# Attention, transforms and the first FFN tiles issued along one written list instead of tables per step

## The chip, the core and the metric

The kernel runs on one core of a Trainium2 chip, as one program. The metric is device time in microseconds, from the launch to the end of the core. In the profile PE is TensorE's matmul side and PEld its weight loads, DVE is VectorE, ACT is ScalarE, POOL is GpSimd and SP is SyncE, which issues most of the DMAs.

## What is computed

Attention with a window of 128 and 4 sink tokens, for 4 batches of 8 heads over 768 tokens, then a Fourier mixing of the result, then a feed-forward network (FFN) with a residual. All in fp32.

```python
keep = is_sink | ((rel >= 0) & (rel < window))          # rel = i - j, sinks are j < 4
a = softmax(where(keep, scale * q @ k.T, -1e9)); x = a @ v   # 4 x 8 heads, S = 768, D = 64
X = fft(fft(x, axis=1), axis=2)                          # over tokens, then over the 512 channels
u = x + real(X)
un = (u - mean(u)) / sqrt(var(u) + 1e-6)
out = u + relu(un @ w_ch1) @ w_ch2                       # 512 -> 2048 -> 512
```

## The kernel before

**Attention.** A query block is 128 tokens; there are 24 (g = 0 to 23, six to a batch). Each block has four steps, one per pair of heads, so that step s stands for block s // 4 and pair s % 4, and 96 steps (and 14 more to drain) make the stage. At even steps `scores` makes the scores of two pairs in a PSUM tile `s` (two buffers). `merge` (VectorE, `copy_predicated`) picks between window and sink columns, `soft1` (VectorE) adds the mask and takes the row's minimum, `expo` (ScalarE) takes the exponential, `sink_p` (GpSimd) splits off the four sink columns. For every second pair `trans_p` turns four heads' weights on TensorE into PSUM tile `pt` (one buffer), `copy_p` (ScalarE) moves them to SBUF as `pta`, `newer_p` and `older_p` (GpSimd) cut them to the two key blocks, and `av` multiplies with V into `xt`. Per block `trans_sink` turns the sink weights, from block 8 on into the same tile `pt`, `copy_sink` moves them, `copy_x` moves `xt`, `turn_x` turns it back and adds the sinks' part, and `store_x` (VectorE) scales it into the token block `u`. A pair of blocks below is written g.pair: `trans_p` 8.3 is that of pairs 2 and 3 of block 8.

**Fourier transform.** When four of a batch's six blocks are stored, `fourier` enters the batch's work in a table `ev` under (step, engine): folds of the token blocks (`fold_n`, `fold_m` on VectorE and GpSimd, `fold_hi` on ScalarE, `fold_lo` on VectorE), stage 1 (`stage1`: products za, za, zr, zb, zb, each in up to two parts), the splits of its results (`z_hi` on ScalarE, `z_lo` on VectorE), stage 2 (`stage2a`, `stage2b`), and `combine` and `update`, which add the result to `u`. Products go to PSUM bank `fft`, or to bank `x` of the attention at certain steps.

**FFN.** 24 token blocks are worked in six groups of four. For an inner tile f (16 of them) `ch1` is 12 matmuls into PSUM tile `h`, `relu` (ScalarE) and `relu_lo` (VectorE) split the result in two, `ch2` is 12 matmuls into four accumulators `o`. `convert` brings a weight tile from 64-bit to 32-bit floats (three VectorE operations, L606 to L608), copies the high part (ScalarE) and subtracts the low one (GpSimd), and issues the next load. The first group runs while the last batches' transforms end. The other five groups run in a loop of their own from some 320 us on (from L1485 on).

**What sets the order.** Each engine works through its own queue in order. Up to step 96 the order is written out: the loop over s issues loads, then `scores`, then for each engine the row of `SCHEDULE[s >= 36]` for s % 4, an operation being called with its lag from `STEP_LAG` or `BLOCK_AT`, and the events of `ev` where the row says so. At `CUT` = 97 `man.close()` ends the written order; from there on the planner of the framework orders all that is issued, by its own costs, until the loop over the other groups, which is written out again. In the row for s % 4 = 3 TensorE has `trans_p`, the events, `av`, `trans_sink`, `turn_x`; `av` falls on even steps alone, so that only events can stand between `trans_p` and `trans_sink`.

## Time and profile before

| | us |
|---|---|
| median of three runs | 760.65 |
| the runs | 757.99, 760.65, 761.95 |
| the profiled execution | 760.99 |
| its span, first to last instruction | 759.3 |
| outside the span | 1.69 |

The profile is of one execution. A busy engine is not an engine at its peak: matmuls are pipelined and their ends are modelled. An idle time is put down to the instruction whose end released the waiting one. A granted clock of 1.00 is 2.4 GHz, one of 0.50 is 1.2 GHz; values between are the mean of a stretch that has both.

### The profile page before, as it was taken

Reading aid. Unit: us, or ns where it says so; the run is one execution under the profiler, and the core shown is the slowest. Engines: PE = TensorE matmul, PEld = TensorE weight load, DVE = VectorE, ACT = ScalarE, POOL = GpSimd, SP = SyncE. Lnnn points to the kernel's source line nnn. Section 1 sums busy time; section 2 is a strip of 40 time slices with the busy share of each in tenths; the row PEclk is TensorE's granted clock in tenths of the full one; section 3 lists DMA queues with packets and bytes.
Section 4 is the critical chain, followed back from the end, with each engine's and each line's share of the span. In section 5 each row is a group of like instructions: output and inputs, shape, how many; then the busy total and the mean of one; then the engine's idle time right before and its main releaser. Section 6 shows DMA issues by size and latency. Waiting matters only on the chain.

```text
span 759.3 us, 14752 instructions
## 1 busy us (share of the span) xinstructions
PE 727.4 (96%) x5223; PEld 626.7 (83%) x5223; DVE 598.6 (79%) x1630; ACT 345.2 (45%) x896; POOL 187.0 (25%) x289
## 2 busy tenths in 40 slices
PE   8987998989899999999999999999999999999995
PEld 6766876867688878788889898898999989898994
DVE  7997688889899789879787798677895798674435
ACT  5885776756543233345555334333443334333330
POOL 3675486577638254200000000000000000000001
PEclk9998999999999999999999999999999999999998
DMA  9982536433215266135447657656666566655761
GB/s 256 286 242 75 150 87 183 128 127 103 94 63 180 103 195 208 56 125 193 154 153 260 212 161 240 220 171 186 200 215 208 177 185 217 191 159 179 217 186 60
DMA packets 95306, 129.18 MB, mean 170 GB/s; under 512 B 5956, under 2 KB 60748, under 8 KB 94968
## 3 DMA queue, kind: packets, MB, share of 16 engines
q1 hardware_dynamic: 94216, 124.00, 51.8%
q0 software_dynamic: 720, 3.76, 1.5%
q8 instruction: 43, 0.70, 0.4%
q10 hardware_dynamic: 288, 0.39, 0.1%
q14 instruction: 39, 0.32, 0.1%
HBM read 104.00 MB, written 24.13 MB: 169 GB/s over the span
## 4 chain that ended last, share of the span: by engine, by line
PE 76%; DVE 16%; issue 2%; DMA 2%; ACT 2%; SPq 1%; POOL 1%; DVEq 0%; ACTq 0%; POOLq 0%
PE h L644 32%; PE p L1360 26%; PE xt L843 4%; PE o L1186 4%; PE s L738 3%; PE pt L805 2%; DVE sm L769 2%; DVE s L753 2%; PE za L402 2%; DVE f L369 1%; DVE gl L385 1%; PE zb L402 1%; DVE f L379 1%; PE a L429 1%; PE zr L402 1%
## 5 line engine op out<-in xcount | busy, mean ns | idle before, releaser
L1360 PE MATMUL p<-w_ring,h_sums 128*128 128x256 f32 x936 | 131.4, 282 | 0.0
L1360 PEld LDWEIGHTS p<-w_ring,h_sums 128*128 128x128 f32 x936 | 123.0, 188 | 3.5 <-DVE u L1190 0.2
L1308 ACT CAST h_sums<-sums 128x256 fp32r<-128x256 f32 (+2 forms) x158 | 89.8, 568 | 68.8 <-PE p L1360 30.6
L1309 DVE TENSOR_TENSOR h_sums<-sums,h_sums 128x256 fp32r<-128x256 f32 (+2 forms) x158 | 98.3, 622 | 17.7 <-ACT h_sums L1308 16.6
L1360 PE MATMUL p<-w2t,h_sums 128*128 128x256 f32 x702 | 110.3, 282 | 0.0
L1382 POOL TENSOR_TENSOR u<-u,u 128x512 f32<-128x512 f32 x3 | 3.8, 1288 | 425.3 <-DVE u L1382 425.3
L1360 PEld LDWEIGHTS p<-w2t,h_sums 128*128 128x128 f32 x702 | 97.6, 189 | 3.4
L644 PE MATMUL h<-un_slots,w 128*128 128x512 f32 x396 | 97.9, 395 | 0.0
L644 PE MATMUL h<-un_last,w 128*128 128x512 f32 x396 | 97.2, 394 | 0.0
L780 ACT ACTIVATE sm<-sm,mx 128x132 f32<-128x132 f32 x192 | 75.9, 399 | 23.0 <-DVE mx L769 22.4
L644 PEld LDWEIGHTS h<-un_slots,w 128*128 128x128 f32 x396 | 72.6, 188 | 15.1
L644 PEld LDWEIGHTS h<-un_last,w 128*128 128x128 f32 x396 | 72.2, 188 | 15.0 <-DVE un_slots L559 0.7
L1522 ACT ACTIVATE sums<-h 128x512 f32<-128x512 f32 x40 | 23.9, 598 | 98.8 <-PE h L644 98.8
L1210 DVE STREAM_TRANSPOSE unf<-un 32x128 f32<-32x128 f32 x192 | 58.0, 302 | 2.8
L1490 ACT ACTIVATE sums<-h 128x512 f32<-128x512 f32 x40 | 23.9, 599 | 67.6 <-PE h L644 67.6
L1319 DVE TENSOR_TENSOR sums<-sums 128x256 f32<-128x256 f32 x39 | 16.4, 421 | 48.4 <-ACT sums L1522 48.1
L769 DVE CUSTOM_DVE_ANT_0 sm<-s,mask 128x132 f32<-128x132 f32 x192 | 47.1, 289 | 3.2 <-DVE s L753 0.5
L843 PE MATMUL xt<-ptl,ldv 128*64 128x128 f32 x384 | 40.5, 297 | 1.0 <-issue 0.9
L738 PE MATMUL s<-ring,q 64*64 64x196 f32 (+1 forms) x640 | 37.7, 351 | 3.0 <-DVE mx L769 2.8
L753 DVE COPY_PREDICATED s<-other,s 64x256 f32<-64x256 uint8 x80 | 34.5, 431 | 5.6 <-PE s L738 2.9
L821 POOL TENSOR_SCALAR_AFFINE_SELECT ptl<-pta 128x512 f32<-128x512 f32 x48 | 32.2, 672 | 22.0 <-ACT pta L812 17.5
L780 ACT ACTIVATION_READ_ACCUMULATOR sm<-sm,mx 128x1 f32 x192 | 36.7, 191 | 0.0
(236 smaller groups left out, 1365.8 us busy)
## 6 DMA issues: line engine op xcount, KB each, us to landing
w_ring<-w2s SPq DMA_DIRECT2D x62, 512.0 KB
w2t<-w2s SPq DMA_DIRECT2D x93, 256.0 KB
raw<-in_moe_w_ch_dram SPq DMA_DIRECT2D x32, 512.0 KB
w2s<-w_ring SPq DMA_DIRECT2D x16, 512.0 KB
ldv<-in_v_dram SPq DMA_DIRECT2D x28, 256.0 KB
ring<-in_qk_dram SPq DMA_DIRECT2D x24, 264.0 KB
w2s<-w2t SPq DMA_DIRECT2D x24, 256.0 KB
out_dram<-u SPq DMA_DIRECT2D x22, 256.0 KB
```

Source lines behind the costliest of these rows:

```text
L402: T.matmul(ps[:, :NK], a, c, start=i == 0, stop=i == len(mm) - 1)
L644: T.matmul(ps[:, :tb], a[:, cs], x[:, :, cc, :], start=n == 0, stop=n == 3 * NCC - 1)
L738: T.matmul(ps[HC * x:HC * x + HC, j, c:c + k.shape[-1]], st["q", g][rows, hp + i, HC * x:HC * x + HC], k, start=True, stop=True)
L753: V.copy_predicated(part(rows, c_out), other[qi > 2][rows], part(rows, c_in))
L769: V.tensor_tensor_reduce(sm[:, h % 4], ps[:, j, c:c + W], mask[min(qi, 3)], -SCALE, 3.0e38, ALU.add, ALU.min, accum_out=mx[:, 0, h:h + 1])
L780: A.activation(sm[:, h % 4], sm[:, h % 4], AF.Exp, bias=mx[:, 0, h:h + 1], scale=-1.0, accum_out=mx[:, 1, h:h + 1])
L821: G.affine_select(lo, a, [[0, 4], [s, P]], compare_op=ALU.is_ge, fill=0.0, base=0, channel_multiplier=-s)
L843: T.matmul(ps[D * j:D * j + D, p, :], st["v", kb(g) - i][:, h, :], a[:, h % 4, :], start=i == 0, stop=i == n - 1)
L1210: V.transpose(unf[32 * q:32 * q + 32, :, r], un[r].rearrange("p (c q j) -> p c q j", c=NCC, q=4)[:, :, q])
L1308: A.copy(hc_hi[:, left(a, n)], src)
L1309: V.tensor_tensor(hc_lo[:, left(a, n)], src, f32(hc_hi[:, left(a, n)]), op=ALU.subtract)
L1360: T.matmul(acc[i][:, 2 * P * tp:2 * P * tp + 2 * P], x, w, start=q == 0 and tp == 0 and n == 0, stop=q == end and n == 2, skip_group_check ...
```

## The change

The loop over the steps no longer issues anything itself. A generator, `everything`, yields the same pieces of work in the order of the tables (each with its step, a name and a function), over all 110 steps and on through the first five inner tiles of the FFN's first group. The pieces are put in queues by a one-letter code (`CODES`), and then a string, `WORK`, of 1158 letters is read from left to right: each letter calls the next piece of its queue. So pieces of one code keep their order, and pieces of different codes stand as the string says. All of this lies within the written order; the planner comes in at the sixth inner tile (`F_LIST` = 5), no longer at step 97.

With it go some smaller edits. Events have more codes (`EVENTS`): the folds' casts are "B", the weight conversions "W", "E" and "I", where `convert` is cut in three (`join`, `join_hi`, `join_lo`), and so on. Which PSUM bank a transform's product takes is a letter too: T for `fft`, X for the attention's `x`, Y for the FFN's `n`; R is a `trans_sink` into `fft`. Tiles are made when their first piece runs (`part_of`, `Made`). The first two inner tiles put their `relu` into buffers of the attention (`pta`, `ptl`), since these are still open. The operations, their shapes and their engines are the same, and there are as many of them. Twelve of the letters T early in the list are pieces that issue nothing (`FILL` = 0), and the letters q near the end load nothing.

An example of how to read it: in the fourth row, `t f a V c G f e r m s` is `trans_p` 8.3, a `soft1`, `av` 8.1, a `fold_m`, `copy_p` 8.3, a `fold_n`, `soft1` 9.1, `expo` 9.0, `trans_sink` 8, `merge` 9.2, `scores` 10.0. By the tables TensorE has `trans_p` 8.3, `trans_sink` 8, `scores` 10.0, `av` 8.1 there, and ScalarE `expo` 9.0, `expo` 9.1, `copy_x` 7, `copy_p` 8.3; by the list ScalarE has `copy_x` 7, `copy_p` 8.3, `expo` 9.0.

```diff
-EVENTS = ("A", 0, 1, 2, 3, "V", "G", "T")
+EVENTS = {"A": "ABCE", 0: (0,), 1: (1,), 2: (), 3: (), "V": "VLOW", "G": "GHI", "T": "TNP"}
...
-ENGINES = ("S", "A", 0, 1, 2, 3, "V", "G", "T")
+ENGINES = ("S", "A", "B", "C", "E", 0, 1, "V", "L", "O", "W", "G", "H", "I", "T", "N", "P")
+F_LIST = 5
 EV_D, EV_Z = 0, 1
 X_AT, X_NOT = (2,), (81, 97)
+EVEN, ODD = ("merge",), ("sink_p", "trans_p", "copy_p", "newer_p", "older_p", "av")
+OLDER, FIRST = ("older_p", "merge"), ("sink_hi", "sink_lo")
+CODES = {
+    "load_qk": "q", "load_k": "k", "load_sink": "n", "load_v": "v", "S": "S", "scores": "s", "merge": "m", "soft1": "f", "expo": "e",
+    "sink_p": "i", "trans_p": "t", "copy_p": "c", "newer_p": "w", "older_p": "o", "av": "a", "copy_x": "x", "copy_sink": "y",
+    "trans_sink": "r", "turn_x": "u", "inverse": "d", "store_x": "z", "sink_hi": "h", "sink_lo": "l", "A": "A", "B": "B", "C": "C",
+    0: "D", 1: "Z", "W": "W", "E": "E", "I": "I", "P": "P", "banks": "0", "second": "1", "third": "3", "keep": "j", "relu": "J", "relu_lo": "K", "ch2": "2",
+    "V": "V", "L": "L", "O": "O", "G": "G", "H": "H", "T": "T", "N": "N", "M": "M",
+}
+OTHER = {"R": "r", "X": "T", "Y": "T"}
+WORK = (
+    "TsTTkqsTqTTvMTTTTTTTTTTTTTCMfeffsefVsveitmeqfcifetwmRscGfyaewftmeisvvcfaefwqVteoscmeitfwxRdyuocfeaiV"
+    "mwesqoftefiVsGzncRGmAeawfyteodvicfxVwsmqeuofhiVeafteVzRsmGciaywfeVdotvfxVmcseuwqfefoamivetzSiRfacdyf"
+    "weskltoxefsqvfuGcVieazAtwefVoRacdyeswftxVoemSuicsfviefawVqeGtzmRaciSyVswSxtfeduGfcamGesvvfBtwfeqVaos"
+    "cVeitxzcwamoRVuGyafedifBTwmeosqvVxitfaVcGfermsnyewztfoucdieafGmesqwvtfBofeViscTzewmxorfyuAidetfacmes"
+    "wqvZhtofiefTzcTmewrfsoAkdayieZXfxlefTfeidTAdeTZtiAucZswqvzTofeVGTfaVAetZiXcdGrsywAaBomtfxTfcewuAsSve"
+    "zTVGqmaDtifXHcfeVTwArsSyDeaVHmtxfTicfHeduAsvvewTzqomaitDGsVHcaBfferVTywxtemuocfsqeiVawfeztomsGnhcafe"
+    "fwmroxvsqyfHuefmetiaHcLesztGLacwfBtdovxfiVcsqweTmveoXLAiZTwforfTAmiyeTZeLaAiufedftezskaLciLwZrsLoqvy"
+    "lxTLfTeftLLXLcfAdwTfeZoaALietZLeLudLLcTizswLroVayGtmxTcufAfwesSvVTezGqmaiBGtVTcXAwfrsDSyeaHfeLtHmxTc"
+    "uLwTfsvvVAeoaVqTiftqqqqqqeDGszciTBHmNrVaCwTyxftedaoOcaGfAeVuwxTmsovDtiLHTfcVeraywfezsotmiGNfcadHCfBO"
+    "seVwuevmTxoLitAafcHerfzysemNwftoCdaciOewfueomsvxiZtLfTcfewzTemoNriafCdAaOyeZtf0edTWciTXAdETwZYoAWITt"
+    "ATcTZErZuAWTwyxTYAaDETzoWaIuxTVYAETITPDVAIVSSTJHPDVHzBKuJVVVVz1V2VBKVV2VVBVVTVV3jjYWAZAEHTZWIYAZEWTA"
+    "IPAZEZWITJYAKETWAPIDEVTJI2AKWHTPDEVIWTJ2AHKETWIDEVIWHEWIEI"
+)
...
+            other_bank = [None]
 
             def bank(b, name):
                 turn[0] += 1
-                if len(banks) == 1 and extra:
-                    t = extra[0](f"{name}_{b}")
-                    if t is not None:
-                        return t
+                if other_bank[0] == "X":
+                    return extra[0](f"{name}_{b}")
+                if other_bank[0]:
+                    pool, t, n = banks[other_bank[0] == "Y"]
+                    return pool.tile([P, 512], F32, tag=t, name=f"{name}_{b}", bufs=n)
                 pool, t, n = banks[turn[0] % len(banks)]
...
-                    at(k + F_S[0], "A", lambda j=j: fold_hi(j))
+                    at(k + F_S[0], "B", lambda j=j: fold_hi(j))
...
-                        pool, tag = (ps_fft, "fft") if NP * g + BLOCK_AT["trans_sink"] < PHASE else (ps_t, "pt")
+                        pool, tag = (ps_fft, "fft") if other_bank[0] == "R" else (ps_t, "pt")
...
-                    at(s + CONV_AT[i], "V", lambda i=i: convert(i))
+                    at(s + CONV_AT[i], "W", lambda i=i: join(i))
+                    at(s + CONV_AT[i] + 1, "E", lambda i=i: join_hi(i))
+                    at(s + CONV_AT[i] + 1, "I", lambda i=i: join_lo(i))
                 for f in range(2):
-                    at(s + CH1_AT[f], "T", lambda f=f: hp.append(ch1(0, f, unT0)))
-
-            hp = []
...
+                    h = [state["aw"].tile([P, tb], F32R, tag=t, name=f"{t}h_{f}", bufs=PTB) for t in ("pta", "ptl")]
...
-                        s = at_s = 0
-                        extra.append(lambda name: ps_t.tile([P, 512], F32, tag="x", name=name)
-                                     if at_s % NP in X_AT and not X_NOT[0] <= at_s <= X_NOT[1] and at_s < len(steps) - 2 else None)
-                        while s < last:
+                        def use(s, op, lag_):
+
+                            if 0 <= s - lag_ < len(steps):
+                                g, hp = steps[s - lag_]
+                                if op not in (EVEN if hp % 2 else ODD) and (g % NB or op not in OLDER):
+                                    yield op, lambda: table[op](g, hp)
+
+                        def use_block(s, op):
+
+                            g, k = divmod(s - BLOCK_AT[op], NP)
+                            if k == 0 and 0 <= g < NQ and (g % NB == 0 and g or op not in FIRST):
+                                yield op, lambda: table[op](g)
+                                if op == "store_x" and g % NB == 3:
+                                    b = g // NB
+                                    fourier(b, lambda d, e, f: at(s + d, e, f), FOLD_AT if b < B - 1 else FOLD_LAST)
+
...
+                        def work(s):
+
+                            yield from loads(s)
+                            yield from events(s, "S")
+                            if s < len(steps) and s % 2 == 0:
+                                yield "scores", lambda: scores(*steps[s])
                             if s == 0:
                                 a, b, e = SINK0_AT
-                                at(a, "A", lambda: sink_hi(0))
+                                at(a, "C", lambda: sink_hi(0))
                                 at(b, e, lambda: sink_lo(0))
                             for e in "AVGT":
-                                for op in SCHEDULE[s >= PHASE][e][k]:
+                                for op in SCHEDULE[s >= PHASE][e][s % NP]:
                                     if op in EVENTS:
-                                        run_ev(s, op)
+                                        for key in EVENTS[op]:
+                                            yield from events(s, key)
                                     elif op in STEP_LAG:
-                                        lag(table[op], s, STEP_LAG[op])
+                                        yield from use(s, op, STEP_LAG[op])
                                     else:
-                                        at_ = s - BLOCK_AT[op]
-                                        if at_ % NP == 0 and 0 <= at_ // NP < NQ:
-                                            table[op](at_ // NP)
-                                            if op == "store_x" and at_ // NP % NB == 3:
-                                                b = at_ // NP // NB
-                                                fourier(b, lambda d, e, f, s=s: at(s + d, e, f), FOLD_AT if b < B - 1 else FOLD_LAST)
-                            run_ev(s, "M")
-                            s += 1
+                                        yield from use_block(s, op)
+                            yield from events(s, "M")
...
+                            yield s, "second", second
+                            for f in range(F_LIST):
+                                if f > 1:
+                                    yield s, "P", lambda f=f: first_product(f)
+
+                                def relu_hi(f=f):
+                                    hs[f] = relu(0, f, hps[f])
+
+                                yield s, "relu", relu_hi
+                                yield s, "relu_lo", lambda f=f: relu_lo(0, hps.pop(f), hs[f])
+                                for _ in range(PER_F):
+                                    for e in ENGINES:
+                                        for op, fn in events(s, e):
+                                            yield s, op, fn
+                                    s += 1
+                                if f < 2 or f > 2:
+                                    j = f if f < 2 else f - 1
+                                    yield s, "ch2", lambda j=j: ch2(j, hs.pop(j), state["po"])
+                                if f == 1:
+                                    yield s, "third", third
+                                    for j in range(2):
+                                        yield s, "keep", lambda j=j: keep_w2(j)
+                                for i in () if f < 1 else range(4, 8) if f == 1 else range(2 * f + 4, 2 * f + 6):
+                                    yield s, "W", lambda i=i: join(i, state["wa"])
+                                    yield s, "E", lambda i=i: join_hi(i, state["wa"])
+                                    yield s, "I", lambda i=i: join_lo(i)
...
+                        for s, op, fn in everything():
+                            queues.setdefault(CODES[op], []).append(fn)
+                            plain.append(CODES[op])
+                            if op == "trans_sink" and s < PHASE:
+                                plain[-1] = "R"
+                            if op == "T" and s % NP in X_AT and not X_NOT[0] <= s <= X_NOT[1] and s < len(steps) - 2:
+                                plain[-1] = "X"
+                            if op == "T" and s > len(steps) + 2 and len(plain) % 2:
+                                plain[-1] = "Y"
+                        todo = {c: iter(q) for c, q in queues.items()}
+                        for c in WORK or plain:
+                            other_bank[0] = c
+                            next(todo[OTHER.get(c, c)])()
+                        other_bank[0] = None
+                        assert all(next(q, None) is None for q in todo.values())
```

## Rows read from the trace of the kernel before

**Rows 1.** The page: its line of busy times, and the granted clock in 40 slices
```profile
PE 727.4 (96%) x5223; PEld 626.7 (83%) x5223; DVE 598.6 (79%) x1630; ACT 345.2 (45%) x896; POOL 187.0 (25%) x289
...
PEclk9998999999999999999999999999999999999998
```

**Rows 2.** Busy time by stretch: PE, PEld, DVE, ACT, POOL, clock, DMA
```profile
0.00:205.00 205.00, 185.13 (x2001) 147.86 (x2001) 171.04 (x685) 141.97 (x527) 128.10 (x244) 0.96 0.53 160
205.00:250.00 45.00, 41.92 (x243) 36.53 (x244) 44.59 (x80) 15.84 (x32) 26.02 (x17) 1.00 0.33 111
...
320.00:759.30 439.30, 431.32 (x2663) 386.51 (x2661) 322.94 (x768) 165.35 (x300) 3.78 (x3) 0.99 0.58 185
```

**Rows 3.** What TensorE waited for until 330 us: total, times, longest
```profile
PE pk L862 <- ACT pta L812: 7.5, 6, 3.2
PE s L738 <- DVE mx L769: 2.8, 3, 1.2
PE a L429 <- DVE d L456: 2.1, 1, 2.1
...
PE a L429 <- DVE mx L769: 1.5, 1, 1.5
PE dc L429 <- DVE zb L417: 1.3, 1, 1.3
```

**Rows 4.** Stretches of 5 us with a low clock, columns as in rows 2
```profile
60.00:65.00 5.00, 1.60 (x17) 1.22 (x17) 4.76 (x21) 3.01 (x11) 3.19 (x9) 0.92 0.54 166
65.00:70.00 5.00, 5.00 (x39) 3.83 (x40) 2.37 (x11) 2.33 (x11) 1.88 (x4) 0.50 0.32 103
...
115.00:120.00 5.00, 2.79 (x37) 2.15 (x37) 4.79 (x24) 3.99 (x15) 4.77 (x11) 0.88 0.54 172
120.00:125.00 5.00, 5.00 (x45) 4.16 (x38) 3.41 (x10) 2.45 (x11) 1.99 (x3) 0.77 0.88 310
165.00:170.00 5.00, 4.95 (x44) 4.22 (x45) 4.21 (x14) 1.82 (x9) 3.98 (x6) 0.66 0.67 209
195.00:200.00 5.00, 3.48 (x25) 2.93 (x25) 4.95 (x17) 3.17 (x12) 3.51 (x4) 0.74 0.32 105
```

**Rows 5.** In order of time, the longest wait: start, us, engine, line, operation
```profile
62.98 0.08 DVE L769 DVE_READ_ACCUMULATOR2_ANT mx<- 128x1 f32 x1
...
64.14 0.58 ACT L812 COPY pta<-pt 128x512 f32<-128x512 f32 x1
...
64.86 0.34 PE L862 MATMUL pk<-ident_r,sk 128*128 128x128 f32 x1 [3.22 <-ACT pta L812]
...
65.13 1.61 PE L738 MATMUL s<-ring,q 64*64 64x196 f32 x16
```

**Rows 6.** One product of AV in the chain; then stage 1's start, batch 0
```profile
78.05 1.02 PE xt L843 x16
...
54.77 0.60 ACT L382 CAST gh<-f 128x512 fp32r<-128x512 f32 x1
...
58.42 0.91 PE L738 MATMUL s<-ring,q 64*64 64x196 f32 x16
```

**Rows 7.** VectorE's subtraction as a group, and one meeting with GpSimd
```profile
L385 DVE TENSOR_TENSOR gl<-f,gh 128x512 fp32r<-128x512 f32 x12 | 12.2, 1017 | 0.1
...
57.80 1.28 POOL L369 TENSOR_TENSOR f<-u 128x512 f32<-128x512 f32 x1
57.85 1.78 DVE L385 TENSOR_TENSOR gl<-f,gh 128x512 fp32r<-128x512 f32 x1
```

**Rows 8.** The start: one load issued, the first exponential, one load in the chain
```profile
4.22 0.62 SPq L707 DMA_DIRECT2D vt<-in_v_sink_dram  x1
...
6.30 0.41 ACT L780 ACTIVATE sm<-sm,mx 128x132 f32<-128x132 f32 x1 [3.91 <-DVE mx L769]
...
9.51 5.15 DMA ldv<-in_v_dram
```

More of the change, by code (lines that the diff above doesn't have):

```diff
@@ L148, with __init__, __missing__ @@
 O_END = O_SM + 2 * 2 * NL
+class Made(dict):
+    def __init__(self, make):
+        self.make = make
+    def __missing__(self, j):
+        self[j] = self.make(j)
+        return self[j]
 def _round12(a):
@@ L609, in convert, with join_hi @@
                 load_w(i + LDB)
-                tf = t.bitcast(F32)
+                state["t", i] = t
+                if which and f < 2:
+                    state["cv", f] = t
+            def join_hi(i, pool=None):
+                f, which = divmod(i, 2)
                 if i < 4:
@@ new lines, in run, with first_product, open_second, open_third @@
+            hps, hs, hc = {}, {}, []
+            def first_product(f):
+                hps[f] = ch1(0, f, unT0)
+            def open_second():
+                state["ps_o"] = ps_o = p1.enter_context(tc.tile_pool(name="ps_o" + tag, bufs=1, space=PSUM, side="right"))
+                state["po"] = [ps_o.tile([P, DM], F32, tag=f"o{i}", name=f"o{i}_0") for i in range(len(groups[0]))]
+            def open_third():
+                state["wa"] = p1.enter_context(tc.tile_pool(name="wa" + tag, bufs=1, side="right"))
+                state["pg"] = ExitStack()
+                state["g0"] = state["pg"].enter_context(tc.tile_pool(name="g0" + tag, bufs=1, side="right"))
@@ new lines, in keep_w2, with relu @@
+            def keep_w2(f):
+                A.copy(w2_raw(f, state["wa"]).bitcast(F32), state.pop(("cv", f)).bitcast(F32))
+            def relu(g, f, ps):
+                tb = P * len(groups[g])
+                if hc:
+                    t = hc[0].rearrange("p i t -> p (i t)")
+                    h = [t[:, 2560 * (f % 2) + 512 * i:2560 * (f % 2) + 512 * i + 512] for i in range(2)]
+                elif "g0" in state:
+                    h = [state["g0"].tile([P, tb], F32R, tag=f"h{i}", name=f"h{i}_{g}_{f}", bufs=2) for i in range(2)]
+                else:
+                    h = [state["aw"].tile([P, tb], F32R, tag=t, name=f"{t}h_{f}", bufs=PTB) for t in ("pta", "ptl")]
+                A.activation(h[0], ps[:, :tb], AF.Relu)
+                return h
@@ new lines, in relu_lo, with ch2 @@
+            def relu_lo(g, ps, h):
+                tb = P * len(groups[g])
+                V.scalar_tensor_tensor(h[1], ps[:, :tb], 0.0, f32(h[0]), op0=ALU.max, op1=ALU.subtract)
+            def ch2(f, h, po, part=slice(None)):
+                w = Wt[f, 1]
+                for i in range(len(po))[part]:
+                    ts_ = slice(P * i, P * i + P)
+                    for n, (a, x) in enumerate(((h[0], w[0]), (h[0], w[1]), (h[1], w[0]))):
+                        T.matmul(po[i], a[:, ts_], x, start=f == 0 and n == 0, stop=f == NF - 1 and n == 2)
@@ L1058, in window_attention, with first_group, second, third @@
-                            run_ev(s, "M")
-                            s += 1
+                                        yield from use_block(s, op)
+                            yield from events(s, "M")
+                        extra.append(lambda name: ps_t.tile([P, 512], F32, tag="x", name=name))
+                        def first_group(s):
+                            def second():
+                                pt.close()
+                                open_second()
+                            def third():
+                                pa.close()
+                                open_third()
+                            yield s, "second", second
[22 more added lines that the diff above has]
+                                    yield s, "I", lambda i=i: join_lo(i)
+                            while ev:
+                                for e in ENGINES:
+                                    for op, fn in events(s, e):
+                                        yield s, op, fn
+                                s += 1
@@ new lines, in banks_of_ffn, with everything @@
+                        def banks_of_ffn():
+                            pb.close()
+                            open_ffn()
+                        def everything():
+                            for s in range(last):
+                                if s == len(steps) + 1:
+                                    start_ffn(s)
+                                    yield s, "banks", banks_of_ffn
+                                for op, fn in work(s):
+                                    yield s, op, fn
+                            yield from first_group(last)
```

153 lines of the change are left out of this document (70 added, 83 removed).

## The prediction

> **What bounds the kernel now.** I read the page first: TensorE is busy for 727.4 of 759.3 us and its granted clock is at full almost throughout, so only its idle time and its slow stretches can be won, unless work is removed, and the change removes none [rows 1]. The busy times by stretch say where: from 320 us on the idle time is 439.3 − 431.3 = 8 us, nearly all at the kernel's very end, and the change doesn't reach there; in the first 205 us TensorE is idle for 20 us at a mean clock of 0.96 [rows 2]. Between 205 and 250 us VectorE is busy for 44.6 of 45 us: there it is the bound, and an order can't shorten its work. In the first 205 us it is busy for 171 us and has room [rows 2].
>
> Then I read what TensorE waits for. The largest group, 7.5 us in six waits, is `trans_sink` (pk) behind ScalarE's `copy_p` (pta): both turns use the one buffer `pt` [rows 3]. The longest of these, 3.22 us, shows the mechanism. ScalarE makes the copy at 64.14, behind exponentials that wait for VectorE; TensorE stands at `trans_sink` until 64.86, with `scores` 10.0 queued behind it, and starts those at 65.13, though VectorE had read the tile that they overwrite at 62.98 + 0.08 = 63.06 [rows 5]. In those five microseconds TensorE is busy for 1.60 us; in the next five its clock is 0.50, which is the 1.2 GHz level, and VectorE, now waiting for scores, is busy for 2.37 us only [rows 4]. A wait of three microseconds so costs nearly as much again in clock. Shorter forms of this stand around 115 and 165 us [rows 4].
>
> **The change part by part.** No operation is added or removed; every term is a wait taken away, kept or made.
>
> *A: the sink's turn.* By the tables only events stand between `trans_p` g.3 and `trans_sink` g, and in most fold stretches there are none. In the list I counted what TensorE has there for the 16 blocks that use `pt`: 0.8 to 3.5 us of work, mostly an `av` of 1.02 us [rows 6], some with scores or a part of stage 1 beside it. At block 8 ScalarE also copies before two exponentials instead of after. At block 14, the second long wait, only TensorE's side is better (two pieces, 1.9 us). Of 7.5 us I take 5.5 away and leave 0.3 for each of six.
>
> *A's clock.* The lost clock is 5 us times one minus the granted clock: 0.40 + 2.50 + 0.60 + 1.15 = 4.65 us for the stretches from 60, 65, 115 and 120 us [rows 4]. They follow from A's two long waits. I take 3.6 away.
>
> *B: products that wait for an eviction.* Stage 2 behind `combine` 2.1 us, behind a minimum 1.5, behind the split of zb 1.3: 4.9 us [rows 3]. In the list the `combine` pieces of batches 1 and 2 stand 2 to 13 places earlier in VectorE's queue, and from the third batch on products change banks by letter. I take half, 2.5 us; the rest lies beside VectorE's full stretch. Their clock is 1.70 + 1.30 = 3.0 us [rows 4]; half, 1.5.
>
> *C: scores behind soft1,* 2.8 us [rows 3]. VectorE's own work ends there; nothing.
>
> *What passes through.* Behind a removed wait the next thing is VectorE. At 65 us scores could have started at 63.06 instead of 65.13: 2.07 of 3.22 us, 0.64. I use that for the waits: (5.5 + 2.5) × 0.64 = 5.1. The clock is lost where TensorE is the bound (VectorE 2.37 of 5 us), so it passes whole: 3.6 + 1.5 = 5.1. Together 10.2 us.
>
> *The start.* The list puts `sink_hi` 0 at the head of ScalarE's queue and `sink_lo` 0 before the first `merge`. Behind the first stands `expo` 0.0, now at 6.30. Its load goes out at 4.22; no row shows it land. The nearest load took 5.15 us [rows 8], so the exponential may go from 6.30 to some 10 us. The cost is between 0 (VectorE puts its masks there meanwhile, which it has to make anyhow) and 3.7 us; I take 1.0, nearer to nothing because three buffers `sm` stand between. The masks move 2 us of VectorE's work ahead, at no cost in sum.
>
> *Loads.* On SP `load_v` now mostly stands behind the following `load_qk`. Whoever is queued behind waits longer by its issue, about 0.6 us [rows 8]. Nothing is taken for it: no load is among TensorE's larger waits [rows 3]. If that cover went, it would be TensorE behind `av`. GpSimd's loads of constants move by three places in its queue, with nothing waiting for them yet.
>
> *The FFN's first tiles.* The planner let conversions run ahead up to the fourteenth tile; the list does the same and puts the last transform earlier among the FFN's matmuls. With VectorE full from 205 to 250 us [rows 2], I take 0 here; the bounds are −2 and +3 us, the size of B's and C's waits [rows 3].
>
> **Sum.** 760.99 − 10.2 + 1.0 = 751.8 us on the profiled execution. That lies 0.34 above the median shown, so I don't correct for it: **752 us**.
>
> **The rivals.**
>
> *More (741 us).* All of A and B pass whole with all their clock: 7.5 + 4.9 + 4.65 + 3.0 = 20 us. For it: VectorE has 34 us of room until 205 us. Against it: in the stretches in question VectorE is busy for 4.76, 4.79 and 4.95 of 5 us [rows 4].
>
> *The same (761 us): VectorE meets GpSimd.* The list pairs folds, updates and subtractions of the two engines anew. The subtraction gl took 1.78 us when it began beside a 1.28 us operation of GpSimd, and ended 0.55 us after that; its mean over 12 is 1.02 [rows 7]. If all twelve met, that were 12 × 0.76 = 9.2 us on the engine that bounds the fold stretches: 751.8 + 9.2 = 761.0. For it: GpSimd's folds stand two to four places later in its queue, next to VectorE's subtractions. Against it: the other direction is as likely. The Trainium skill, page "SBUF — State Buffer", section "Who interferes with whom", says that a VectorE instruction with two SBUF inputs and a GpSimd instruction that reads SBUF exclude each other for their whole length; the meeting above agrees.
>
> *Slower (770 us): stage 1 in front of scores.* In the list the first part of za stands before `trans_p` and scores in three batches; by the tables it stands behind. It needs the folds of two blocks. If they come late, TensorE holds the scores back, and VectorE starves in turn. The price of one such place is the longest wait with its clock, 3.2 + 2.9 = 6.1 us [rows 4, 5]; three are 18.4: 751.8 + 18.4 = 770.2. It decides from two places on (764.1). Against it: in batch 0 the second cast ended at 54.77 + 0.60, 3.05 us before the scores 9.2 that now follow the part [rows 6]. For it: a faster TensorE arrives earlier, while the folds are VectorE's and come no sooner.
>
> *The list doesn't do what it says (761 us):* the pieces of an engine keep nearly their old order, so that it might change nothing. The moves around `trans_sink` speak against it.
>
> **How the numbers follow.** The forecast has 0.55, more 0.13, the meetings 0.17, stage 1 in front 0.12, no effect 0.03. What a measurement tells from no change is about 0.5%, 3.8 us, or 756.8 to 764.5. So faster 0.68, the same 0.20, slower 0.12. The range goes from 742, where most of "more" ends, to 763, which takes in the meetings and the bounds of the start and the FFN; it leaves out the slow case and the last of the fast one.
>
> **What would show it.** Right: pk's waits behind pta below 3 us in sum, no stretch at 0.50 after 60 us, the last `scores` earlier than now by about 9 us, and an idle time of TensorE until 205 us near 12 us. The pass-through is right if scores then wait for soft1 longer than 2.8 us. Wrong: new long waits of za behind gh or gl (stage 1 in front), a mean of gl above 1.3 us (the meetings), the first `av` later by over 2 us (the start), or a gain before 205 us that VectorE's full stretch gives back after it.

## The result and the profile after

| | before | after |
|---|---|---|
| median, us | 759.75 (757.99 to 761.95) | 747.36 (746.89 to 747.70) |
| profiled execution, us | 760.99 | 747.41 |
| its span, us | 759.3 | 745.6 |

The median before is now of four runs: the three shown above and one of 758.84 us. The ratio is 0.9835, with a 95% interval of 0.9806 to 0.9864: 12.5 us faster. The forecast was 752.0 us in a range of 742 to 763, which holds it. The sum behind it, though, is wrong in two places that partly cancel: the gain before 205 us is twice the forecast's, and some 9 us of it are lost again behind, where the forecast took nothing.

The page of the changed kernel, its line of TensorE's busy time and the granted clock in 40 slices, against [rows 1]:

```profile
PE 722.8 (97%) x5223; PEld 622.8 (84%) x5223; DVE 593.8 (80%) x1630; ACT 344.0 (46%) x896; POOL 180.3 (24%) x289
...
PEclk9999999999999899999999999999999999999998
```

Busy time by stretch, after, columns as in [rows 2] (PE, PEld, DVE, ACT, POOL, clock, DMA):

```profile
0.00:205.00 205.00, 198.87 (x2140) 160.82 (x2141) 181.18 (x716) 146.75 (x540) 131.49 (x250) 1.00 0.53 160
205.00:250.00 45.00, 37.28 (x182) 30.82 (x181) 42.29 (x78) 12.95 (x25) 23.01 (x19) 0.95 0.50 163
...
320.00:745.60 425.60, 418.10 (x2603) 375.74 (x2602) 316.51 (x753) 159.66 (x290) 3.79 (x3) 0.99 0.58 188
```

In the first 205 us TensorE is idle for 6.1 us instead of 19.9, and the slow stretches of [rows 4], together 7.65 us of lost clock, are gone: 13.7 + 7.7 = 21.4 us. The last `scores` start at 168.21 instead of 190.25 us. Some 9 us of this are lost again before the FFN runs evenly: the first matmul of its tile 7 (`ch1` 7) starts at 254.53 instead of 267.80, only 13.3 us earlier, and that is what is left at the end. The last `scores` and this matmul, first before, then after:

```profile
190.25 0.91 PE L738 MATMUL s<-ring,q 64*64 64x196 f32 x16
267.80 0.74 PE L644 MATMUL h<-un_slots,w_gh 128*128 128x512 f32 x2
...
168.21 0.91 PE L842 MATMUL s<-ring,q 64*64 64x196 f32 x16
254.53 0.62 PE L700 MATMUL h<-un_slots,w_gh 128*128 128x512 f32 x2
```

What TensorE waited for until 330 us, after, against [rows 3]:

```profile
PE h L700 <- POOL w_gl L690: 2.8, 1, 2.8
PE warm L1037 <- POOL ident masks.py:199: 1.9, 1, 1.9
PE o L760 <- DVE us L972: 1.9, 1, 1.9
PE a L470 <- DVE d L498: 1.7, 1, 1.7
PE h L700 <- ACT w_gh L683: 1.5, 1, 1.5
...
PE s L842 <- DVE mx L871: 0.2, 1, 0.2
PE pk L962 <- POOL sk L894: 0.2, 1, 0.2
```

`trans_sink` (pk) no longer waits for `copy_p` (pta) at all: 7.5 us before. Scores wait for soft1 for 0.2 us: 2.8 before. The wait called warm stands at the very start, as before. The other large ones stand behind 195 us, around the last transform and the FFN's first tiles; the largest is for a weight (h behind w_gl).

Block 8, where the longest wait of [rows 5] stood, in order of time, after:

```profile
59.28 0.44 PE L943 MATMUL xt<-ptl,ldv 128*64 128x128 f32 x4
59.39 0.58 ACT L914 COPY pta<-pt 128x512 f32<-128x512 f32 x1 [1.24 <-PE pt L907]
...
60.31 0.28 PE L962 MATMUL pk<-ident_r,sk 128*128 128x128 f32 x1
...
60.81 0.91 PE L842 MATMUL s<-ring,q 64*64 64x196 f32 x16 [0.22 <-DVE mx L871]
```

TensorE makes an `av` while ScalarE makes the copy, in front of the two exponentials instead of behind them; `trans_sink` goes without a wait, and `scores` 10.0 start at 60.81 instead of 65.13.

And the place where TensorE loses most now, 242 to 247 us, with the 5 us stretches around it:

```profile
242.81 0.62 ACT L683 CAST w_gh<-cv 128x512 fp32r<-128x512 f32 x1 [2.90 <-DVE cv L655]
243.18 0.76 POOL L508 TENSOR_TENSOR us<-us,d 128x257 f32<-128x257 f32 x1 [3.09 <-DVE d L506]
243.90 1.33 POOL L509 TENSOR_TENSOR us<-us,d 128x255 f32<-128x255 f32 x1
245.19 1.79 POOL L690 TENSOR_TENSOR w_gl<-cv,w_gh 128x512 fp32r<-128x512 f32 x1
...
247.03 0.79 PE L700 MATMUL h<-un_slots,w_gl 128*128 128x512 f32 x1 [2.81 <-POOL w_gl L690]
```

```profile
240.00:245.00 5.00, 2.73 (x11) 1.61 (x9) 4.91 (x10) 0.62 (x1) 1.91 (x3) 1.00 0.51 182
245.00:250.00 5.00, 2.97 (x7) 2.39 (x8) 2.83 (x5) 1.16 (x2) 4.45 (x4) 0.53 0.81 289
250.00:255.00 5.00, 5.00 (x19) 3.98 (x19) 2.54 (x4) 1.22 (x2) 0.54 (x1) 0.79 0.11 22
```

The weight tile could have been made from 243.4 us, when its cast ended. GpSimd stood in the last update of the fourth batch until 245.2. TensorE waits for 1.5 and 2.8 us, and its clock then falls to 0.53 and 0.79: 2.35 + 1.05 = 3.4 us more.

### The profile page after: what moved, and what is told of

It reads as the page before. It is cut to its first block, busy times and chain, and to the rows that moved or that the text cites. A ratio compares the mean times of both kernels' runs of the same rounds, so it can differ in the third digit from the quotient of the medians.

```text
span 745.6 us, 14718 instructions
## 1 busy us (share of the span) xinstructions
PE 722.8 (97%) x5223; PEld 622.8 (84%) x5223; DVE 593.8 (80%) x1630; ACT 344.0 (46%) x896; POOL 180.3 (24%) x289
## 4 chain that ended last, share of the span: by engine, by line
PE 81%; DVE 11%; ACT 3%; issue 1%; DMA 1%; POOL 1%; SPq 0%; DVEq 0%; ACTq 0%
PE h L700 34%; PE p L1526 26%; PE xt L943 5%; PE o L760 3%; PE s L842 3%; PE pt L907 3%; ACT sm L882 2%; PE x L955 1%; PE a L470 1%; PE b L492 1%; PE zb L443 1%; PE za L443 1%; DVE cv L654 1%; DMA vt<-in_v_sink_dram 1%; PE x L957 1%
## 5 line engine op out<-in xcount | busy, mean ns | idle before, releaser
L1475 DVE TENSOR_TENSOR h_sums<-sums,h_sums 128x256 fp32r<-128x256 f32 (+2 forms) x158 | 98.3, 622 | 17.5 <-ACT h_sums L1474 16.3
L943 PE MATMUL xt<-ptl,ldv 128*64 128x128 f32 x384 | 38.3, 285 | 0.0
L842 PE MATMUL s<-ring,q 64*64 64x200 f32 (+1 forms) x640 | 36.1, 340 | 0.2 <-DVE mx L871 0.2
```

Of the source, the lines that this page charges most:

```text
L842: T.matmul(ps[HC * x:HC * x + HC, j, c:c + k.shape[-1]], st["q", g][rows, hp + i, HC * x:HC * x + HC], k, start=True, stop=True)
L943: T.matmul(ps[D * j:D * j + D, p, :], st["v", kb(g) - i][:, h, :], a[:, h % 4, :], start=i == 0, stop=i == n - 1)
L1475: V.tensor_tensor(hc_lo[:, left(a, n)], src, f32(hc_hi[:, left(a, n)]), op=ALU.subtract)
```

## The experiments

The theory: the gain is part A's, `trans_sink` no longer holds TensorE's queue, and behind the attention stage VectorE, which is full there, gives some of it back. Rivals: the smaller edits or the missing planner make the difference; no single place does; the list's own tail loses what is lost. Ratios are to the kernel before, run beside it.

**The tables' order, through the changed kernel.**

```diff
+                        order = plain
-                        for c in WORK or plain:
+                        for c in order:
```

> The same pieces in the order of the tables (the list is not used; PSUM banks by the tables' own rule), all of it written out, so that the planner doesn't order the steps from 97 on. Theory: the written order makes the gain. Then this kernel loses it: 756 to 766 us, TensorE's waits for pta at trans_sink again 6 to 9 us in sum, its mean clock until 205 us again about 0.96, last scores near 190 us. Rival (the other edits, or the missing planner, make the gain): 745 to 751 us, last scores near 168 us.

Measured: 778.26 us, ratio 1.0206 (1.0165 to 1.0247), worse than either case. TensorE's waits until 205 us are those of [rows 3] again (pk behind pta 6.9, scores behind soft1 2.8), and the last `scores` start at 190.46. So far the theory holds. But the kernel is 16 us behind the kernel before by the ratio (18 by the medians), and all of that arises later: with no planner, the tables' order behind step 97 leaves TensorE 1.31 us busy from 210 to 215 us, with VectorE busy for 3.81 of these 5 us, and a clock of 0.50 after it. The prediction's "there it is the bound, and an order can't shorten its work" was too simple: an order can leave VectorE idle there.

**The planner put back, with the tables and with the list.** Both close the written order where the kernel before did:

```diff
                             other_bank[0] = c
+                            if c == "0":
+                                man.close()
```

> The tables' order up to the piece that opens the FFN's PSUM banks, and the planner for all that follows, as in the kernel before, but made by the changed kernel's generator with all its smaller edits (codes, convert in three pieces, tiles made when first used). Theory: these edits cost and bring nothing, 757 to 764 us, and the 18 us by which the tables kernel was slower than the kernel before are the planner's work behind step 97. Rival (the edits themselves cost some of the 18 us, by tiles and banks taken in another order): 766 to 778 us.

Measured: 761.36 us, 1.0034 (1.0011 to 1.0056). The smaller edits gain nothing; if anything they cost 2.6 us. The planner's work behind step 97 is worth 1.0206 − 1.0034 = 1.7%, 13 us. This is the base for the next runs.

> The list up to the same piece (978 of 1158), then the planner, as in the kernel before. Theory: VectorE is full behind the attention stage, so that whoever orders that part ends it at much the same time: 744 to 751 us, FFN tile ch1_7 at 252 to 258 us. Rival 1 (the list's last 180 pieces give away 9 us that the planner would keep): the planner needs 77.5 us from the last scores to ch1_7, as in the kernel before, which gives ch1_7 near 246 us and 738 to 742 us. Rival 2 (the planner's order is worse): above 752 us.

Here the order starts as `WORK[:WORK.index("0") + 1]` (979 letters) and goes on with what is left of `plain`. Measured: 745.36 us, 0.9824 (0.9801 to 0.9847), which can't be told from the changed kernel's 0.9835; `ch1` 7 starts at 253.15. As the theory has it, the list's last 179 pieces end at the same time as the planner's order. They don't get there the same way: with the planner the last `scores` start at 172.01, 3.8 us later, and from there to `ch1` 7 it needs 81.1 us where the list needs 86.3 (77.6 in the kernel before). So the list's end gives away some 5 us that the planner keeps, and the planner loses nearly as much in front. The gain, 1.0034 − 0.9824 = 2.1% or 16 us, is that of the order up to that letter.

> The list up to the piece that opens the FFN's PSUM banks (piece 978 of 1158), the rest in the order of the tables, without the planner. Theory: the gain is made in the attention stage and about 9 us are given back behind it whatever the order there, because VectorE is full: last scores near 168 us and 745 to 753 us. Rival 1 (the list's own last 180 pieces give the 9 us back): 738 to 744 us. Rival 2 (the list's last 180 pieces hold the FFN's start together, the tables' order there is bad): above 754 us with long waits of h for converted weights.

The same without the planner. Measured: 763.36 us, 1.0037 (1.0015 to 1.0059): rival 2. TensorE's waits from 170 to 250 us, the first three:

```profile
PE a L470 <- DVE d L498: 7.5, 1, 7.5
PE zb L443 <- DVE zr L455: 3.2, 2, 2.1
PE h L700 <- ACT w L683: 2.2, 2, 1.8
```

Against the changed kernel it loses 15 us, the whole gain. With this order behind it a faster attention stage is worth nothing; it needs the list's own end or the planner behind it.

**Part A undone in the list.** What TensorE has between `trans_p` g.3 and `trans_sink` g stands behind it, in blocks 8 to 14 and 16 to 23. Two of the places, block 8 (a, an `av`, goes behind r) and block 12 (X and T, two products of stage 2, go behind with the copy A):

```diff
-... sqvVxitfaVcGfermsnyew ...
+... sqvVxitfVcGferamsnyew ...
...
-... aDtifXHcfeVTwArsSyDea ...
+... aDtifHcfeVwrXTAsSyDea ...
```

> The list with part A undone in blocks 8 to 14 and 16 to 23: what TensorE has between trans_p g.3 and trans_sink g (one to three pieces, with what hangs on them) stands behind trans_sink; everything else is the list's. Theory: the waits for pta return (5 to 9 us in sum) and the kernel is 4 to 10 us slower than the changed one, 751 to 757 us. Rival (the copy's earlier place on ScalarE, or the slack elsewhere in the list, carries the gain): waits for pta below 2.5 us, 746 to 749.5 us.

Measured: 763.08 us, 1.0033 (1.0017 to 1.0050): 15.0 us slower than the changed kernel, more than the theory's 4 to 10. What TensorE waits for until 205 us:

```profile
PE pk L962 <- ACT pta L914: 10.1, 12, 1.1
PE pk L962 <- POOL sk L894: 2.3, 2, 1.9
...
PE pt L907 <- ACT pta L914: 1.4, 1, 1.4
```

The waits return, now in twelve places, each of 1.1 us or less, because the edit takes away more than the tables lacked. The last `scores` come at 182.04, 13.8 us later than in the changed kernel. Up to its last `scores` TensorE is idle for 16.2 us instead of 3.9, which is 12.4 of these 13.8 us: in the list the waits pass almost whole. The granted clock stays at 1.00 until 205 us, so that the clock has no part in it.

**Part A alone, in the tables.** Three forms. The first puts both `av` g.1 and `scores` g+2.0 in front of `trans_sink` g (base: the tables kernel, 778.26 us), the second only `av` (its loop moves `("a", 2 * g)` alone; base: tables_planner, 761.36 us):

```diff
+                        for g in range(8, NQ):
+                            for c, n in (("s", 2 * (g + 2)), ("a", 2 * g)):
+                                ...
+                                r, i = find(order, "r", g), find(order, c, n)
+                                order.insert(r, order.pop(i))
```

> The tables' order with one change: from block 8 on, av g.1 and scores g+2.0 stand before trans_sink g instead of behind it. Theory, as forecast for part A: the waits for pta fall below 2.5 us, and with their low-clock stretches this is worth 4 to 10 us against the tables kernel, so about half of what the list gains before 205 us. Rival (no single place carries the gain, TensorE only meets the next wait, for soft1 or for folds): within 2 us of the tables kernel, and scores wait longer for soft1.

Measured: 775.34 us, 1.0186 (1.0151 to 1.0221): no gain that can be told from the base. pk's waits for pta are gone, but the following turn takes their place, and scores wait longer:

```profile
PE pt L907 <- ACT skt L967: 5.3, 15, 0.4
PE s L842 <- DVE mx L871: 5.2, 5, 1.5
```

The buffer `pt` passes from `trans_p` g.3 to `trans_sink` g to `trans_p` g+1.1, and behind each there is a copy. Two pieces in front of `trans_sink` leave none behind it.

> The tables_planner kernel (761.4 us) with only av g.1 in front of trans_sink g from block 8 on, scores g+2.0 staying behind it, so that both turns of the shared buffer have cover. Theory: an av of about 1 us takes most of the short waits for pta and a third of the long ones: pk's waits 2 to 4 us, 754 to 758 us. Rival (the cover is missed on the other side, as in tables_A, where 15 turns waited 5.3 us for the copy of the sink; or VectorE is next): 759 to 763 us.

Measured: 759.70 us, 1.0013 (0.9993 to 1.0034), 1.6 us better than its base by the ratios, with overlapping intervals: the rival. pk's waits are down to 1.0 us, the last `scores` at 184.70 instead of 189.39, but `av` itself now waits for GpSimd's pieces:

```profile
PE xt L943 <- POOL sk L893: 3.0, 2, 2.7
PE xt L943 <- POOL pta L929: 3.0, 3, 2.2
PE s L842 <- DVE mx L871: 2.8, 3, 1.2
```

The third form changes no queue. In four blocks `trans_sink` takes another bank, and so need not wait for the copy that empties `pt`:

```diff
-                            if op == "trans_sink" and s < PHASE:
+                            if op == "trans_sink" and (s < PHASE or s // NP - 1 in (8, 13, 14, 20)):
                                 plain[-1] = "R"
```

> The tables_planner kernel (761.4 us) with one letter changed: in blocks 8, 13, 14 and 20, where nothing of TensorE's stood between trans_p g.3 and trans_sink g, trans_sink takes the bank fft instead of pt, so that it no longer has to wait for copy_p; every queue keeps its order. Theory, part A of the forecast by its full size: the waits of pk behind pta fall from 7.6 to under 1 us, the half clock after 65 us and at 120 us goes with them, and the kernel takes 750 to 755 us. Rival (behind the removed wait stands the next one, as the pass-through of 0.64 or less says, and most of the list's gain is elsewhere): 756.5 to 761 us, with scores waiting longer than 2.8 us for soft1.

Measured: 756.65 us, 0.9985 (0.9964 to 1.0007); by the ratios 0.5%, 3.7 us, better than its base: the rival. TensorE's waits until 205 us, two groups of them, and a pair of slow stretches:

```profile
PE s L842 <- DVE mx L871: 4.5, 5, 1.4
...
PE pk L962 <- ACT pta L914: 0.6, 2, 0.3
```

```profile
60.00:65.00 5.00, 3.12 (x40) 2.41 (x42) 4.76 (x21) 3.03 (x11) 3.19 (x9) 0.92 0.53 172
65.00:70.00 5.00, 5.00 (x36) 4.34 (x36) 3.24 (x15) 3.31 (x16) 3.13 (x6) 0.74 0.30 97
```

pk's waits fall by 7.0 us. Scores then wait for soft1 for 4.5 us instead of 2.8, the clock still falls behind the place (and for 5 us at 160 us to 0.68, where the base kept 1.00), and the last `scores` start 4.8 us earlier (184.60). This is what the forecast said of part A alone, a part passes and VectorE is next, but it is about a quarter of the 16 us that the list gains over the same base.

**The letters of the banks.** The order stays; 15 letters of transform products change (6 from Y, the second bank behind the opening, to T; 9 between T and X), and five of pieces that only warm TensorE or do nothing. One stretch of it:

```diff
-... TcTZErZuAWTwyxTYAaDETzoWaIuxTVYAETITPDV ...
+... TcTZErZuAWTwyxTTAaDETzoWaIuxTVTAETITPDV ...
```

> The changed kernel with the PSUM banks of the transforms' products chosen by the tables' rule: 20 of the list's letters T, X and Y changed, 15 of them at products of the transforms; the order stays. Theory: TensorE's products hardly wait for a bank in the list, so the letters are worth little, 746.5 to 749 us. Rival (the banks by letter carry part B of the forecast, 2.5 us with 1.5 us of clock): 750 to 752 us, with stage 2 waiting for combine or for a copy.

The text expects the tables' rule. As run, the kernel has no Y at all, so that after the FFN's banks open all products of stages 1 and 2 share one bank. Measured: 763.52 us, 1.0078 (1.0048 to 1.0109), 2.4% or 18 us slower than the changed kernel and far beyond both cases. `scores` 9.2 start as in the changed kernel (57.88 and 57.86 us), so the five letters of warming or empty pieces cost nothing. Until the last `scores` (171.30) it loses 3.1 us, the size that the rival gives to part B. The other 15 us come behind, where products wait for the eviction of the one before, for example:

```profile
181.02 0.62 PE L443 MATMUL zb<-cst,gh 128*128 128x386 f32 x2 [1.45 <-DVE zr L455]
184.63 0.62 PE L443 MATMUL zb<-cst,gh 128*128 128x386 f32 x2 [1.75 <-DVE zb L457]
```

```profile
170.00:205.00 35.00, 29.50 (x218) 24.85 (x215) 22.20 (x59) 14.85 (x47) 16.70 (x23) 0.90 0.33 114
```

**What is given back behind 205 us.** Two attempts to keep other work out of the way of the weight pieces. The first issues the rest of the first group as written, so that the planner can't slip the second group's LayerNorm forward:

```diff
-CUT, MAN0 = 97, False
+CUT, MAN0 = 97, True
```

> The list as it is; the first FFN group behind it is issued as written instead of by the planner, which so can no longer slip the second group's LayerNorm (some 7 us of VectorE between 205 and 227 us) in front of the list's weight joins. Theory: the joins of tile 6 come up to 7 us earlier, the waits of h at 243 and 247 us (4.3 us) and the half clock behind them (3.4 us) go: 740 to 745 us. Rival (the order as written serves the rest of the group worse, or the LayerNorm comes too late for the second group): 748 to 760 us with waits of h or unt behind 255 us.

Measured: 764.90 us, 1.0068 (1.0046 to 1.0090): the rival, by more than it says. The waits for weights fall only from 4.3 to 3.1 us, and the LayerNorm now comes too late:

```profile
PE unt L592 <- DVE un L586: 15.8, 2, 10.8
PE h L700 <- POOL w_gl L690: 2.3, 1, 2.3
```

`ch1` 7 does start earlier, at 251.62 instead of 254.53, so the planner's slipping may be some 3 us of the 9. But without the planner the second group loses more than it wins: the kernel is some 17 us slower.

The second moves two letters, an update each on VectorE and GpSimd, which nothing needs until much later:

```diff
-    "IPAZEZWITJYAKETWAPIDEVTJI2AKWHTPDEVIWTJ2AHKETWIDEVIWHEWIEI"
+    "IPAZEZWITJYAKETWAPIDEVTJI2AKWHTPDEVIWTJ2AHKETWIDEIWEWIEIVH"
```

> The list with its last two updates of the fourth batch (update 0.0 on VectorE, update 0.1 on GpSimd) moved to its end, behind the last weight pieces. Theory: in the changed kernel GpSimd made update 0.1 from 243.18 to 245.23 while w_gl was ready to be made from 243.4; with it behind, w_gl comes 1.8 us earlier and TensorE waits 1 to 1.8 us less at 247 us, with less half clock behind: 744 to 746.5 us. Rival (VectorE's joins are what ends last there, GpSimd's place in the queue doesn't matter): 746.8 to 748 us.

Measured: 743.75 us (742.53 to 743.94), 0.9796 (0.9777 to 0.9814): the fastest of all and just below the theory's 744 to 746.5. It is 3.6 us below the changed kernel's median, with no run of the one within the other's; by the ratios 3.0 us, with intervals that just meet. The place of 247.03:

```profile
241.35 0.62 ACT L683 CAST w_gh<-cv 128x512 fp32r<-128x512 f32 x1 [2.74 <-DVE cv L655]
242.05 1.27 POOL L690 TENSOR_TENSOR w_gl<-cv,w_gh 128x512 fp32r<-128x512 f32 x1 [2.01 <-ACT w_gh L683]
...
243.38 0.50 PE L700 MATMUL h<-un_slots,w_gl 128*128 128x512 f32 x1 [0.62 <-POOL w_gl L690]
```

w_gl is begun 3.1 us earlier. Both moves count: the cast in front of it comes 1.5 us earlier, since VectorE's update no longer stands in front of the join, and GpSimd begins 0.08 us behind the cast instead of 1.76. TensorE's wait of 2.81 is one of 0.62 us, and the clock stays at 1.00. So of the 9 us given back, about 3 were the place of two pieces in the list.

> The changed kernel with all six updates of the fourth batch (three on VectorE, three on GpSimd) at the end of the list, behind the last weight pieces. Theory: VectorE is what ends last until 250 us, and each update taken out of its queue there (1.9 us) brings the joins behind it forward: 741 to 743 us, below the 743.75 of the kernel with one pair moved. Rival (TensorE's remaining waits there are for combine and for GpSimd, or the second group's LayerNorm comes too late): 743.5 to 747 us.

```diff
-    "IPAZEZWITJYAKETWAPIDEVTJI2AKWHTPDEVIWTJ2AHKETWIDEVIWHEWIEI"
+    "IPAZEZWITJYAKETWAPIDETJI2AKWTPDEIWTJ2AKETWIDEIWEWIEIVHVHVH"
```

Measured: 744.78 us, 0.9831 (0.9785 to 0.9877): the rival. TensorE there waits for w_gh for 3.2 us, and the clock falls to 0.73 after 250 us. More of the same gives nothing that shows.

## Why the prediction was right or wrong

**What bounds the kernel** was read rightly: what could be won before 205 us, the idle time and the slow stretches, is what was won. But the signs named for it were too modest: an idle time near 12 us (6.1 came), the last `scores` 9 us earlier (22 came). The sign named for the pass-through came out the other way: scores were to wait for soft1 longer than 2.8 us, and wait for 0.2.

**A, the sink's turn.** The direction was right, the size too small: 5.5 of 7.5 us were to go, all 7.5 went. The clock: 3.6 of 4.65 us were to come back, all came, with that of part B. One reading was off: the stretch around 165 us is no shorter form of A's waits. TensorE's wait there, which ended at 165.05 us, was one of 2.08 us for d; the sum rightly counts its clock under B.

**B.** Half of 4.9 us and of 3.0 us of clock were forecast. Two of the three groups of [rows 3], 3.6 us, stood before 205 us, and are gone. The third ended at 206.03 us, and behind 205 us the changed kernel still has such waits, the largest 1.7 us (a behind d, above). The run with other letters puts the part of the letters, until the last `scores`, at about 3 us. That is a rough figure: the last `scores` of the runs that keep the letters start between 168.20 and 169.42 us, and at 172.01 where the planner follows.

**C** was taken as nothing, "VectorE's own work ends there". That failed: 2.8 us became 0.2. At the longest of these waits (1.17 us, until 54.64) VectorE had made a subtraction, a fold and `store_x`, from 51.89 to 53.73 us, in front of the last four soft1. In the changed kernel the four soft1 at this place start at 49.93 us and the subtraction behind them, at 51.10. It was VectorE's own work, as the forecast says, but in an order that could be changed. This was not tried by itself.

**What passes through** is the step that failed most. One place, scores that could start 2.07 us before they did, gave 0.64 for all waits. For part A alone the figure is of the right kind: with 7.0 us of pk's waits removed (tables_R) the last `scores` came 4.8 us earlier, clock and all, and 3.7 us were left at the end, less than the 7.1 us that the sum has for A with its clock, since scores then waited 1.7 us longer for soft1 and the clock fell again. But the list doesn't remove one kind of wait; it removes nearly all at once, and then little is next. The four kernels in which part A and the rest of the list are there or not:

| | `trans_sink` held back by the copy | not held back | difference |
|---|---|---|---|
| tables, then planner | 761.36 | 756.65 (another bank) | 0.5%, 3.7 us |
| list | 763.08 | 747.36 | 2.0%, 15.0 us |

The differences are by the ratios. Without part A the rest of the list gains nothing; with it, 1.5% or 11 us more than part A brings alone (0.9985 to 0.9835). A sum of terms, each with its own share passing, can't give that. The comparison is not quite clean: the undone list has twelve waits where the tables have six, and products of stage 2 moved with them. Which of the list's other moves make up the 11 us has not been taken apart beyond the letters. The traces name a candidate on VectorE, whose waits the prediction didn't read. Until 205 us `store_x` stood in its queue waiting for `turn_x` for 16.3 us in the kernel before and for 9.6 in tables_R, but for 2.9 in the undone list and 1.6 in the changed kernel. Whatever stood behind `store_x` in that queue, soft1 too, waited with it. No run changes this alone.

**The start.** The first exponential moved from 6.30 to 9.64 us, behind a load that landed at 9.12, within the "6.30 to some 10" of the forecast:

```profile
9.12 0.62 ACT L816 CAST vs<-vt 128x512 fp32r<-128x512 f32 x1 [6.72 <-DMA vt<-in_v_sink_dram]
9.64 0.40 ACT L882 ACTIVATE sm<-sm,mx 128x132 f32<-128x132 f32 x1
```

The first `av` is 0.7 us later (14.86 instead of 14.19), `scores` 6.0 at 36.63 instead of 36.49: the term of 1.0 is 0.1 us by then.

**Loads** were taken at nothing, and none is among TensorE's waits after.

**The FFN's first tiles** were taken at 0, with bounds of −2 and +3 us; it was about +9. The forecast named the mechanism, "a gain before 205 us that VectorE's full stretch gives back after it", as a sign that it is wrong, but did not price it. A stage that ends 22 us earlier hands its successor the same VectorE work in less time: VectorE is busy for 42.3 of 45 us, and TensorE idle for 7.7 instead of 3.1. Up to `ch1` 7 VectorE has nearly the same to do in both, 228.0 us before and 225.5 after; behind the last `scores` it is busy for 78.4 of 86.3 us (69.3 of 77.6 before). So the forecast could have priced a bound from VectorE's work up to the last weight piece. The order matters beside it: two updates moved give back about 3 us. How the rest divides is not shown.

So the sum was 10.2 us of gain and 1.0 of cost against 21.4 and about 9. That 752.0 came out only 4.6 us from 747.4 is in part luck: an error of 11 us met one of 8 the other way.

**The rivals.** *Slower, stage 1 in front of scores:* no product za waits for gh or gl in the list; the folds came in time, at no price that shows. *The same, VectorE meets GpSimd:* the subtraction gl fell instead, from 1017 ns [rows 7] to

```profile
L425 DVE TENSOR_TENSOR gl<-f,gh 128x512 fp32r<-128x512 f32 x12 | 9.1, 755 | 0.9 <-ACT gh L422 0.9
```

3.1 us less on VectorE: here an order did shorten its work. "The other direction is as likely", the forecast said; it was the one. In the tail it went the rival's way (below). *More,* 741 us: before 205 us it was nearly that, 21.4 us against its 20, though with C's wait in place of a part of B's. *Not doing what it says:* the tables' order in the same kernel, 761.36 us with the planner, excludes it.

## What to carry to other kernels

Where an in-order engine is held back in several places, the places are not a sum: taking one away lets the next wait grow, and here only the order that removed nearly all of them let the engine's own work set the pace. Cover both turns of a shared one-buffer tile, the wait for it and the wait behind it, and check that the cover doesn't wait for a third engine. When a stage is made faster, look first at the following one: there two updates that nobody needs yet cost about 3 us, because a weight stood behind them.

## What was not expected of the hardware

*Short pauses and the clock.* With part A undone TensorE was idle for 17.9 of the first 205 us, in waits of up to 1.89 us, and its granted clock was 1.00 throughout. In tables_R a wait of 1.42 us with two shorter ones around it, 3.12 of 5 us busy, was followed by 0.74 (the stretches shown with that run). The longest waits were followed by a slow stretch in both kernels (3.22 us before, 2.81 after), but the length of one pause, or the busy share of 5 us, doesn't tell the two short cases apart.

*VectorE beside GpSimd, in the tail.* The fourth batch's updates on VectorE took 1516 ns on average, where the same form takes 419 ns in an earlier batch:

```profile
L509 DVE TENSOR_TENSOR us<-us,d 128x255 f32<-128x255 f32 x3 | 4.5, 1516 | 0.0
L509 DVE TENSOR_TENSOR u<-u,d 128x255 f32<-128x255 f32 x3 | 1.3, 419 | 0.0
```

One of the three, with the GpSimd operation that runs beside it:

```profile
223.95 1.42 POOL L690 TENSOR_TENSOR w<-cv,w 128x512 fp32r<-128x512 f32 x1 [2.47 <-ACT w L683]
224.14 1.52 DVE L509 TENSOR_TENSOR us<-us,d 128x255 f32<-128x255 f32 x1
```

GpSimd's operation began 0.19 us earlier and ended at 225.37, VectorE's at 225.66, 0.29 us behind it; the other two ended 0.28 us behind theirs. The order by hand puts update and weight piece beside each other each time, for 3 × 1.1 = 3.3 us of a full VectorE. In the kernel before the same three took 708 ns on average, so the list added 2.4 us here. The Trainium skill, page "SBUF — State Buffer", section "Who interferes with whom", has it that a VectorE instruction with two SBUF inputs contends with a GpSimd instruction that reads SBUF, that the ports they share are an exclusive lock, and that the order of issue decides which of the two is blocked; these rows agree.
